# Batch 7's way through memory, in pieces between the layers of the token network, in an attention and mixture-of-depths kernel

## The chip, the cores and the metric

The kernel runs on one core of one Trainium2 chip, in float32. The metric is device time in microseconds (us), from launch to end; lower is better.

A core has five engines, each with its own queue of instructions in a fixed order: PE (matrix products), DVE (vector work, and transposes of 32 x 32 blocks), ACT (activation functions and copies), POOL (vector work, and the DMAs whose rows are picked by an index), SP (all other DMAs here). They wait for each other through semaphores. SBUF is the memory on the core, PSUM the memory that PE writes its products to, DRAM the large one.

## The reference

Attention over 8 batches of 8 heads with queries averaged in pairs, and behind it a mixture of depths: of a batch's 576 rows the 128 with the highest scores go through a two-layer network.

```python
q_pool = q.reshape(B, H, S // 2, 2, D).mean(axis=3)          # B 8, H 8, S 1152, D 64
attn = softmax(q_pool @ k^T / sqrt(D))
x = (attn @ v).transpose(0, 2, 1, 3).reshape(8, 576, 512)
scores = np.einsum('bsd,d->bs', x, w_gate)
out = x.copy()
for b in range(8):
    top_idx = np.argpartition(-scores[b], 128)[:128]
    xe = x[b, top_idx]
    ye = np.maximum(xe @ w1, 0.0) @ w2                        # 512 -> 1024 -> 512
    g = 1.0 / (1.0 + np.exp(-scores[b, top_idx]))
    out[b, top_idx] = x[b, top_idx] + g[:, None] * ye
```

## The kernel before

The order of work on every engine is the order in which the program issues it: the whole of `run` is under a manual schedule, with no planner behind it.

**Attention.** `run` (L1634) goes over 32 pairs of heads, each in two halves of 288 queries. In a half PE makes the scores (L886) and the weighted values of the half before (L904), ACT takes exponents (L893), POOL and DVE the sums. The output rows `x` are stored to `out` in DRAM by SP (L1040).

**Routing.** When a batch's last pair has its scores, a generator `routed(b, part)` (L1074) starts. It issues a few instructions, yields, and is taken up again at set places, so that its pieces stand between other work. Its stages:

- the scores are added up (`line` L1084, `groups` on ACT L955, `total` L961), written to DRAM (L1098) and read back as a line on every partition (L1101);
- ranking: for each of 5 tiles of rows, two DVE passes over the line count how many scores are larger (L1129); POOL and ACT form the gate (L1112, L1142 or L1121, L1145);
- search: which row has rank r. Batches 0 to 6 write rank and gate to DRAM (`row_rank`, L1160), read all of it back to every partition (`lines`, L1164), and let DVE compare (`search`, L1203). Batch 7 instead makes five comparisons (L1173), multiplies them with a table of rows and gates on PE (L1184), turns the result with one more matmul (L1195), and copies index and gate out on ACT (L1196, L1197);
- fetch: POOL gathers the 128 chosen rows from `out` by index (L1230) to `xe`;
- turn: the network needs the rows with features on partitions (`xeT`). Batches 0 to 6 write `xe` to DRAM in an order of its own (L1244), read it back (L1261), and DVE transposes blocks (L1269). Batch 7 is transposed by PE (L1279) and copied by ACT (L1280).

Batches 0 to 5 do all this during the attention, batch 6 mostly; its last pieces and all of batch 7's come in `ending`.

**The network.** The 8 batches are taken in four pairs: (0,1), (2,3), (4,5), (6,7). Each layer of a pair is made as a 2 x 2 product of blocks with seven products instead of eight. The first layer (`first_layer`, L1354) issues seven products of 16 matmuls (L1333), the second (`second_of`, L1426) seven of 8 (L1343). Sums around the products: of the inputs on POOL (`input_sums`, L1319), of the hidden values on DVE (`four_sums`, L1424), and of products on DVE (L1352), with ReLU on ACT (L1368) and copies on ACT (L1370, L1376, L1435, L1437). Every product goes to one of four PSUM tiles, taken in turn (`banks`, L1071); a fifth waits until the first is emptied. At a pair's end DVE scales and adds the result to `xe` (L1347) and POOL scatters it to `out` (`written`, L1302). The hidden quarter c12 is the second operand that the second layer reads, c11 the first.

**The ending.** `ending` (L1456) writes the order out by hand with `pieces(unit, n)`, which takes the next n pieces of a generator: `old` is batch 6's routing, `new` batch 7's, `layer` and `second` pair 0's layers, `third` the next pair's first layer. Pair 0's first layer keeps one product back (`kept`), so that its order is different from the other pairs', and pair 1's first products stand between pair 0's second ones, to fill PE while batch 7 is ranked, searched and turned. Batch 7's routing is done before pair 1 proper begins. In the fourth pair, DVE also checks that all sums of exponents lie in bounds (`counted`, L1592), a small matmul adds the counts (`outside`, L1607), and each engine loads the result (`count_i`, L1560) ahead of the last layer, to branch to a general version if one is out of bounds.

Of the kernel before, what the change touches and what calls it, by code (L numbers as in the profile page):

```python
# [539 lines left out]
class _Plain:  # L540
# [85 lines left out]
    def constants(self):  # L626
# [27 lines left out]
        self.meta = self.const.tile([P, self.NT], F32, name="meta")  # L654
        nc.gpsimd.tensor_scalar(
            out=self.meta[:, :],
            in0=self.token[:, :],
            scalar1=float((self.B - 1) * self.Sp),
            scalar2=None,
            op0=ALU.add,  # L660
        )

# [407 lines left out]

    def banks(self):  # L1071
        return self.psum.tile([P, 2, 512], F32, name="ps")

    def routed(self, b, part):  # L1074
# [33 lines left out]
        if b < self.B - 2:  # L1108
            yield True
        gate = ffn.tile([P, NT], F32, name="gate")  # L1110
# [9 lines left out]
        if b == self.B - 1:  # L1120
            nc.scalar.activation(gate[:, :], gate[:, :], AF.Exp, scale=-1.0)  # L1121
            yield True
        rank = ffn.tile([P, NT], F32, name="rank")
        cuts = {self.B - 2: (1,), self.B - 1: (NT,)}.get(b, (1, 3))
        for t, rows in tiles:
# [12 lines left out]
            if t == cuts[0] < cuts[-1]:  # L1138
                yield True
# [8 lines left out]
        if b == self.B - 1:  # L1148
            meta = self.late[:, self.Dm : self.Dm + NT * BLK].rearrange("p (t n) -> p t n", n=BLK)
            nc.gpsimd.memset(meta, 0.0)  # L1150
            nc.gpsimd.tensor_copy(meta[:, :, 0], self.meta[:, :])
            nc.vector.reciprocal(meta[:, :, 1], gate[:, :])
            nc.vector.tensor_reduce(rank[:, :], parts[:, :, :], AX.X, ALU.add)
        else:

            both = ffn.tile([P, 2, NT], F32, name="both")
            nc.vector.reciprocal(both[:, 1, :], gate[:, :])
            nc.vector.tensor_reduce(both[:, 0, :], parts[:, :, :], AX.X, ALU.add)
            row = self.dram.tile([P * 2 * NT], F32, name="row_rank")
            nc.sync.dma_start(  # L1160
                row.rearrange("(p x) -> p x", p=P), both.rearrange("p a t -> p (a t)")
            )
            lines = ffn.tile([P, P, 2, NT], F32, name="lines", bufs=1)
            nc.sync.dma_start(lines.rearrange("p i a t -> p (i a t)"), _rows_of(row[:], P))  # L1164

        for s0, w in self.slots:
            index = ffn.tile([P, 1], I32, name="index", bufs=self.B)
            own_gate = ffn.tile([P, 1], F32, name="own_gate", bufs=self.B)
            if b == self.B - 1:

                pick = ffn.tile([P, NT, P], F32, name="pick", bufs=1)
                for t, rows in tiles:
                    nc.vector.tensor_scalar(  # L1173
                        out=pick[0:rows, t, 0:w],
                        in0=self.token_line[0:rows, 0, s0 : s0 + w],
                        scalar1=rank[0:rows, t : t + 1],
                        scalar2=None,
                        op0=ALU.is_equal,
                    )
                yield True  # L1180
                ps = self.banks()[:, 0, :]
                n = P // BLK
                for t, rows in tiles:
                    nc.tensor.matmul(  # L1184
                        ps[t % n * BLK : (t % n + 1) * BLK, 0:w],
                        lhsT=meta[0:rows, t, :],
                        rhs=pick[0:rows, t, 0:w],
                        start=(t < n),
                        stop=(t >= NT - n),
                    )  # L1190
                found = ffn.tile([P, NT, P], F32, name="pick", bufs=1)[:, 0, 0:w]
                nc.scalar.copy(found, ps[:, 0:w])
                yield True
                ps = self.banks()[:, 0, 0:2]
                nc.tensor.matmul(ps[0:w, :], lhsT=found, rhs=self.same[:, 0:2], start=True, stop=True)  # L1195
                nc.scalar.copy(index[0:w, :], ps[0:w, 0:1])  # L1196
                nc.scalar.copy(own_gate[0:w, :], ps[0:w, 1:2])  # L1197
            else:
                yield True

                def search(of, to):
                    at = ffn.tile([P, NT, P], F32, name="pick", bufs=1)
                    nc.vector.scalar_tensor_tensor(  # L1203
                        out=at.rearrange("p t i -> p (t i)").rearrange("p (i t) -> p i t", t=NT)[0:w],
                        in0=lines[0:w, :, 0, :],
                        scalar=self.token[0:w, s0 // P : s0 // P + 1],
                        in1=of[0:w, :, :],
                        op0=ALU.is_equal,
                        op1=ALU.mult,
                        accum_out=to[0:w, :],  # L1210
                    )

                found = self.small.tile([P, 1], F32, name="found_token")
                search(self.token_line.rearrange("p t i -> p i t"), found)
                nc.vector.tensor_scalar(
                    out=index[0:w, :],
                    in0=found[0:w, :],
                    scalar1=float(b * Sp),
                    scalar2=None,
                    op0=ALU.add,  # L1220
                )
                if b == self.B - 2:
                    search(lines[:, :, 1, :], own_gate)

                yield True
            if b == self.B - 1:
                xe = ffn.tile([P, self.Dm], F32, name="lines", bufs=1)
            else:
                xe = ffn.tile([P, self.Dm], F32, name="xe", bufs=self.paired + 1)
# [10 lines left out]
            if b != self.B - 1:  # L1240

                n = P // BLK
                copy = self.dram.tile([n, P, P], F32, name="copy")
                nc.sync.dma_start(  # L1244
                    copy[:, 0:w, :].rearrange("a s m -> s a m"), xe[0:w, :].rearrange("s (a m) -> s a m", a=n)
                )
            if b < self.B - 2:
                search(lines[:, :, 1, :], own_gate)
            if b < self.paired:
                xeT = ffn.tile([P, self.ND, P], F32, name="xeT", bufs=self.paired)  # L1250
            if b != self.B - 1:
                yield True
                moved = []

                def read():
                    if b == self.B - 2:
                        moved.append(self.early[:, self.Dm : 2 * self.Dm])
                    else:
                        room = ffn.tile([P, NT, P], F32, name="pick", bufs=1)
                        moved.append(room.rearrange("p t n -> p (t n)")[:, 0 : self.Dm])  # L1260
                    nc.sync.dma_start(moved[0], copy.rearrange("a (j b) m -> (a j) (b m)", b=n))  # L1261

                if b < self.B - 2:
                    self.behind_keys.append(read)
                else:
                    xeT = self.lines_of(self.early[:, 0 : self.Dm])
                    read()
                yield "sums" if b < self.B - 2 else True
                nc.vector.transpose(  # L1269
                    xeT.rearrange("p c (j b) -> p c b j", b=n),  # L1270
                    moved[0].rearrange("p (b i c) -> p c b i", b=n, c=self.ND),
                )
            else:
                yield mid
                xeT = self.lines_of(self.late[:, 0 : self.Dm])
                pv = self.banks()[:, 0, :].rearrange("p (c n) -> p c n", n=P)
                of = xe.rearrange("p (n c) -> p c n", c=self.ND)
                for c in range(self.ND):
                    nc.tensor.transpose(pv[:, c, 0:w], of[0:w, c], self.ident[0:w, 0:w])  # L1279
                nc.scalar.copy(xeT[:, :, 0:w], pv[:, 0 : self.ND, 0:w])  # L1280
# [30 lines left out]
    def input_sums(self, a, s):  # L1311

        a11, a12, a21, a22 = a
        s1, s2, s3, s4 = s
        add, subtract = ALU.add, ALU.subtract
        for i, (to, x, y, op) in enumerate(
            ((s1, a21, a22, add), (s2, s1, a11, subtract), (s3, a11, a21, subtract), (s4, a12, s2, subtract))
        ):
            self.nc.gpsimd.tensor_tensor(out=to, in0=x, in1=y, op=op)  # L1319
            if i % 2:  # L1320
                yield
# [32 lines left out]
    def first_layer(self, a, s, c, m, kept=None):  # L1354


# [15 lines left out]
        ps = product(a12, b21)  # L1372
        yield
        hidden(c11, u, ps)
# [10 lines left out]
        if kept is None:  # L1385
            hidden(c21, u, product(a22, t4))
            yield
# [68 lines left out]
    def ending(self, halves, old):  # L1456
# [6 lines left out]
        def pieces(unit, n=None):  # L1463
            for i, _ in enumerate(unit):
                if i + 1 == n:
                    break
# [308 lines left out]
```

## Time and profile before

| | |
|---|---|
| device time, three runs | 678.05, 680.55, 680.17 us, median 680.17 |
| the profiled execution's own time | 678.44 us |
| its span (first to last instruction) | 676.6 us |
| granted PE clock | 0.998 of full |
| attention's last product on PE begins | 559.66 us (140 matmuls shown from there) |
| pair 0's first product | 568.26 us |
| batch 7: `line` on DVE, gather on POOL, transposes on PE | 575.07, 593.48, 598.13 us |
| last product on PE | 667.39 us, 16 matmuls in 3.62 us |

The span counts from the first instruction of the program; the device time has a little more around it (678.44 against 676.6). "PE" rows are matmuls, "x16" means sixteen of them in the row's time; a bracket at a row's end is the idle time before it and what ended it. "SPq" and "POOLq" are the sequencers of SP and POOL, which issue DMAs.

### The profile page before, as it was taken

Reading aid. Unit: us, or ns where it says so; the run is one execution under the profiler, and the core shown is the slowest. Engines: PE = TensorE matmul, PEld = TensorE weight load, DVE = VectorE, ACT = ScalarE, POOL = GpSimd, SP = SyncE. Lnnn points to the kernel's source line nnn. Section 1 sums busy time; section 2 is a strip of 40 time slices with the busy share of each in tenths; the row PEclk is TensorE's granted clock in tenths of the full one; section 3 lists DMA queues with packets and bytes.
Section 4 is the critical chain, followed back from the end, with each engine's and each line's share of the span. In section 5 each row is a group of like instructions: output and inputs, shape, how many; then the busy total and the mean of one; then the engine's idle time right before and its main releaser. Section 6 shows DMA issues by size and latency. Waiting matters only on the chain.

```text
span 676.6 us, 23416 instructions
## 1 busy us (share of the span) xinstructions
PE 668.3 (99%) x9951; PEld 445.9 (66%) x9951; DVE 564.1 (83%) x824; ACT 448.2 (66%) x978; POOL 502.7 (74%) x476
## 2 busy tenths in 40 slices
PE   9999999999999999999999999999999999999996
PEld 5656666666666666666666666656666667899995
DVE  4878898998999888998799889988998897865464
ACT  6677777777877777777777777777777773321210
POOL 5888888889888978898889988898889878230211
PEclk9999999999999999999999999999999999999999
DMA  8799999858885788768885788678958744310000
GB/s 162 145 199 184 203 183 192 159 106 186 159 161 100 138 166 164 136 116 163 153 166 110 157 153 154 127 148 157 153 127 151 156 132 133 61 48 16 17 32 35
DMA packets 390089, 91.51 MB, mean 135 GB/s; under 512 B 371416, under 2 KB 375384, under 8 KB 389976
## 3 DMA queue, kind: packets, MB, share of 16 engines
q1 hardware_dynamic: 388536, 85.54, 65.8%
q0 software_dynamic: 1280, 4.20, 1.7%
q8 instruction: 79, 1.29, 0.9%
q14 instruction: 34, 0.28, 0.2%
q10 hardware_dynamic: 160, 0.20, 0.1%
HBM read 74.38 MB, written 15.52 MB: 133 GB/s over the span
## 4 chain that ended last, share of the span: by engine, by line
PE 94%; issue 2%; DVE 1%; DMA 1%; POOL 1%; ACT 0%; POOLq 0%; ACTq 0%; DVEq 0%
PE ps L886 42%; PE ps L904 41%; PE ps L1343 5%; PE ps L1333 5%; DMA p<-in_q_dram 0%; POOL p L1319 0%; DMA out_dram<-lines,index 0%; DVE p L1352 0%; POOL prod L993 0%; DVE acc L1352 0%; PE ps L1184 0%; POOL out_dram L1302 0%; PE ps L852 0%; DVE x L1029 0%; ACT groups L955 0%
## 5 line engine op out<-in xcount | busy, mean ns | idle before, releaser
L893 ACT ACTIVATE p<-ps 128x576 f32<-128x576 f32 x576 | 320.8, 694 | 2.7 <-PE ps L886 2.6
L925 POOL TENSOR_TENSOR acc<-p 128x576 f32<-128x576 f32 x192 | 283.1, 1503 | 37.8 <-ACT p L893 37.1
L886 PE MATMUL ps<-qT,kT 64*64 64x288 f32 x4608 | 292.5, 403 | 0.2
L904 PE MATMUL ps<-p,v_sb 64*64 64x288 f32 x4608 | 291.0, 403 | 0.0
L886 PEld LDWEIGHTS ps<-qT,kT 64*64 64x64 f32 x4608 | 174.0, 133 | 106.1 <-ACT p L893 14.6
L904 PEld LDWEIGHTS ps<-p,v_sb 64*64 64x64 f32 x4608 | 172.9, 133 | 106.8 <-ACT p L893 14.9
L930 DVE TRANSPOSE_TENSOR_REDUCE fold<-p 128x54 f32<-128x1728 f32 x64 | 126.2, 1972 | 45.7 <-ACT p L893 45.6
L912 ACT COPY two<-ps 128x576 f32<-128x576 f32 x64 | 41.0, 640 | 132.0 <-PE ps L904 129.5
L930 DVE TRANSPOSE_TENSOR_REDUCE fold<-acc 128x54 f32<-128x1728 f32 x64 | 124.4, 1943 | 4.4 <-POOL acc L925 4.4
L914 POOL TENSOR_TENSOR av<-two 128x288 f32<-128x288 f32 x64 | 51.4, 803 | 39.4 <-ACT two L912 38.7
L774 DVE STREAM_TRANSPOSE kT<-kb 128x1152 f32<-128x1152 f32 x31 | 73.5, 2372 | 0.0
L993 POOL TENSOR_TENSOR prod<-avb,w_gate 128x288 f32<-128x288 f32 x64 | 51.8, 809 | 0.0
L771 POOL TENSOR_TENSOR qp<-qb 128x576 f32<-128x576 f32 (+1 forms) x32 | 43.9, 1374 | 5.7 <-DMA qb<-in_q_dram 5.7
L1129 DVE TENSOR_SCALAR_CACHE_REDUCE pick<-line 128x127 f32<-128x127 f32 (+4 forms) x80 | 45.2, 565 | 2.3
L1302 POOL DMA_INDIRECT out_dram<-xe,index x7 | 7.0, 994 | 47.4 <-DVE xe L1347 38.5
L970 ACT ACTIVATE sums<-total,tiny 32x18 f32<-32x18 f32 x124 | 38.3, 309 | 1.9
L1029 POOL TENSOR_TENSOR x<-avb,rec 128x576 f32<-128x576 f32 x30 | 34.8, 1160 | 0.0
L983 DVE STREAM_TRANSPOSE avb<-av 128x288 f32<-128x288 f32 x64 | 28.4, 444 | 3.2 <-POOL av L914 3.2
L1368 ACT ACTIVATE p<-p 128x512 f32<-128x512 f32 x16 | 10.1, 632 | 31.6 <-DVE p L1352 31.6
L1051 DVE TENSOR_REDUCE red<-prod 128x9 f32<-128x288 f32 x64 | 27.8, 435 | 2.7 <-POOL prod L993 2.7
L955 ACT COPY groups<-sum 32x36 f32<-32x36 f32 x124 | 27.3, 220 | 2.2 <-DVE sum L940 0.7
L779 DVE STREAM_TRANSPOSE qT<-qp 128x576 f32<-128x576 f32 (+1 forms) x32 | 23.4, 732 | 0.7 <-POOL qp L771 0.7
(131 smaller groups left out, 434.7 us busy)
## 6 DMA issues: line engine op xcount, KB each, us to landing
kb<-in_k_dram SPq DMA_DIRECT2D x124, 144.0 KB, 4.8
qb<-in_q_dram SPq DMA_DIRECT2D x124, 144.0 KB, 4.7
v_sb<-in_v_dram SPq DMA_DIRECT2D x31, 576.0 KB, 5.8
out_dram<-x SPq DMA_DIRECT2D x128, 72.0 KB, 5.0
lines<-row_rank SPq DMA_DIRECT2D x7, 640.0 KB
w<-in_moe_w_dram SPq DMA_DIRECT2D x8, 512.0 KB
line<-gate_lines SPq DMA_DIRECT2D x8, 351.5 KB
tw<-tw SPq DMA_DIRECT2D x4, 512.0 KB
```

The lines of the kernel that those rows point to most:

```text
L771: nc.gpsimd.tensor_tensor(out=qp[:, of, :], in0=pair["q"][:, of, 0, :], in1=pair["q"][:, of, 1, :], op=ALU.add)
L774: nc.vector.transpose(kT.rearrange("p (c i g) -> p c g i", c=self.NC, i=BLK), pair["k"].rearrange("p (g c) d -> p c g d", c=self.NC),)
L886: nc.tensor.matmul(sc[keys, j, 0:n], lhsT=pair["kT"][rows, c * P + keys.start : c * P + keys.stop], rhs=pair["qT"][rows, qs], start=True, ...
L893: nc.scalar.activation(p[:, c // G, c % G, :, :], sc[:, :, 0:n], AF.Exp, scale=self.scale)
L904: nc.tensor.matmul(av[j * self.D : (j + 1) * self.D, e, 0:n], lhsT=half["pair"]["v"][keys, j, c, :], rhs=half["p"][keys, c // G, c % G, j, :],
L912: nc.scalar.copy(two[:, :, :], av[:, :, 0:n])
L914: nc.gpsimd.tensor_tensor(out=half["av"][:, :], in0=two[:, 0, :], in1=two[:, 1, :], op=ALU.add)
L925: nc.gpsimd.tensor_tensor(out=acc[:, u, :], in0=units[:, 0, u, :], in1=units[:, 1, u, :], op=ALU.add)
L930: nc.vector.tensor_reduce(fold[:, a, :], of.rearrange("p u (m d) -> p (u m) d", d=BLK), AX.X, ALU.add, apply_transpose=True,)
L970: self.nc.scalar.activation(tot[rows, :], pair["total"][:, j * self.QB : (j + 1) * self.QB], AF.Identity, bias=self.tiny[0:BLK, 0:1],)
L993: self.nc.gpsimd.tensor_tensor(out=pair["prod"][:, ns, :], in0=pair["avb"][:, ns, :], in1=self.w_gate[:, hp : hp + 1, :].broadcast_to([P, ...
L1129: nc.vector.tensor_scalar(out=cmp[0:rows, 0 : part.stop - part.start], in0=near[0:rows, part], scalar1=sc[0:rows, t : t + 1], scalar2=None ...
```

## The change

Batch 7 takes the same way as the other batches: rank and gate to DRAM, lines back, DVE search, gather, copy to DRAM, read back, DVE transpose. The matmuls, the table `meta` and the ACT copies of the other way go. `ending` no longer writes out the order: the routing generators stand in a list `waiting`, and after every piece of a layer `pieces` takes one piece of the first of them. `pause(n)` in `routed` makes batch 7 let n such turns pass. Pair 0 is treated like pairs 1 and 2, in one loop: first layer, one piece of the second, `four_sums`, next pair's `input_sums`, the other pieces. `first_layer` has no `kept` product any more, and seven pieces instead of eight. Before the third pair's last pieces, whatever is left of the routing is issued at once.

```diff
+    def pause(self, n):
+        for _ in range(n):
+            yield True
...
         yield True
         if b < self.B - 2:
             yield True
+        if b == self.B - 1:
+            yield from self.pause(3)
         gate = ffn.tile([P, NT], F32, name="gate")
...
-        if b == self.B - 1:
-            nc.scalar.activation(gate[:, :], gate[:, :], AF.Exp, scale=-1.0)
-            yield True
         rank = ffn.tile([P, NT], F32, name="rank")
-        cuts = {self.B - 2: (1,), self.B - 1: (NT,)}.get(b, (1, 3))
+        cuts = {self.B - 2: (1,), self.B - 1: (0, 1, 2, 3)}.get(b, (1, 3))
...
-            if t == cuts[0] < cuts[-1]:
+            if t in cuts[:-1]:
                 yield True
...
         for s0, w in self.slots:
...
-                for t, rows in tiles:
-                    nc.tensor.matmul(
-                        ps[t % n * BLK : (t % n + 1) * BLK, 0:w],
-                        lhsT=meta[0:rows, t, :],
-                        rhs=pick[0:rows, t, 0:w],
...
+            yield True
             if b == self.B - 1:
+                yield from self.pause(4)
...
             if b == self.B - 1:
-                xe = ffn.tile([P, self.Dm], F32, name="lines", bufs=1)
+                xe = self.late[:, self.Dm : 2 * self.Dm]
...
+            if b < self.B - 2:
+                self.behind_keys.append(read)
             else:
-                yield mid
-                xeT = self.lines_of(self.late[:, 0 : self.Dm])
-                pv = self.banks()[:, 0, :].rearrange("p (c n) -> p c n", n=P)
-                of = xe.rearrange("p (n c) -> p c n", c=self.ND)
-                for c in range(self.ND):
-                    nc.tensor.transpose(pv[:, c, 0:w], of[0:w, c], self.ident[0:w, 0:w])
-                nc.scalar.copy(xeT[:, :, 0:w], pv[:, 0 : self.ND, 0:w])
+                read()
+            yield "sums" if b < self.B - 2 else True
+            if b == self.B - 1:
+                yield from self.pause(3)
+            nc.vector.transpose(
+                xeT.rearrange("p c (j b) -> p c b j", b=n),
+                moved[0].rearrange("p (b i c) -> p c b i", b=n, c=self.ND),
+            )
...
-    def first_layer(self, a, s, c, m, kept=None):
+    def first_layer(self, a, s, c, m):
...
-        ps = product(a12, b21)
-        yield
-        hidden(c11, u, ps)
+        hidden(c11, u, product(a12, b21))
...
-        if kept is None:
-            hidden(c21, u, product(a22, t4))
-            yield
+        hidden(c21, u, product(a22, t4))
+        yield
         hidden(c12, w, product(s4, b22))
         yield
-        if kept is not None:
-            copy(kept, product(a22, t4))
-            yield
-            hidden(c21, u, kept)
-            yield
...
+        waiting = [old]
 
         def pieces(unit, n=None):
             for i, _ in enumerate(unit):
+                while waiting and next(waiting[0], None) is None:
+                    waiting.pop(0)
                 if i + 1 == n:
                     break
...
         self.gated(halves[-3])
-        pieces(old, 1)
+        next(old)
...
-        pieces(layer, 1)
+        pieces(following[4], 1)
         self.normalized(last)
         self.gated(halves[-1])
         self.scored(halves[-1])
         _, new, _ = self.routing.pop()
-        pieces(old, 1)
-        pieces(new, 1)
-        pieces(layer, 3)
+        waiting.append(new)
+        pieces(following[4], 1)
         for of in (halves[-3]["pair"], last):
             self.divided(of)
             self.stored(of)
-        pieces(layer, 1)
-        pieces(old)
-        pieces(layer, 1)
-        pieces(new, 1)
-        pieces(layer, 2)
...
-        for i in range(1, self.B // 2 - 1):
+
+        for i in range(1, self.B // 2):
             tokens, c, s, _, layer = following
             pieces(layer)
-            following = layers(i + 1, rooms[(i + 1) % 2], m[(i + 1) % 2])
-            pieces(self.input_sums(*following[3]))
             second = self.second_of(tokens, c, s, acc[1])
-            pieces(second, 3)
+            pieces(second, 1)
             self.four_sums(c, s)
+            if i == self.B // 2 - 1:
+                while waiting:
+                    for _ in waiting.pop(0):
+                        pass
+            following = layers(i, rooms[i % 2], m[i % 2])
+            self.input_sums(*following[3])
             pieces(second)
 
         (six, seven), c, s, _, third = following
         pieces(third, 4)
         low = self.counted()
         pieces(third, 2)
         count = self.outside(low)
-        pieces(third, 1)
         self.four_sums(c, s, slice(0, 3))
         pieces(third)
         self.four_sums(c, s, slice(3, 4))
```

## The prediction

> **What bounds the kernel now.** First the page's busy shares and the chain that ended last, then each engine's timeline from 568 us on. The order of instructions, which lists for both kernels what stands on each engine and which semaphores it waits for, shows that up to there nothing moves except one small POOL instruction (`meta`) that goes.
>
> ```profile
> PE 668.3 (99%) x9951; PEld 445.9 (66%) x9951; DVE 564.1 (83%) x824; ACT 448.2 (66%) x978; POOL 502.7 (74%) x476
> PE 94%; issue 2%; DVE 1%; DMA 1%; POOL 1%; ACT 0%; POOLq 0%; ACTq 0%; DVEq 0%
> ```
>
> PE works 99% of the span, so only what PE executes, or waits for, sets the time. I number a pair's products F1 to F7 (first layer) and S1 to S7 (second layer) in PE's order; the layers multiply pair 0 from 568.26. PE's timeline:
>
> ```profile
> 568.26 2.05 PE L1333 MATMUL ps<-xeT,w 128*128 128x128 f32 x16
> ...
> 581.09 1.89 PE L1343 MATMUL ps<-w,p 128*128 128x256 f32 x8
> 583.63 1.99 PE L1343 MATMUL ps<-w,p 128*128 128x256 f32 x8 [0.64 <-ACT p L1368]
> ...
> 589.67 1.23 PE L1184 MATMUL ps<-pick,v_sb 128*32 128x128 f32 x10 [0.54 <-ACT acc L1435]
> 590.83 2.05 PE L1333 MATMUL ps<-xeT,w 128*128 128x128 f32 x16
> 592.72 0.28 PE L1195 MATMUL ps<-same,pick 128*128 128x2 f32 x2
> ...
> 598.13 0.63 PE L1279 MATMUL ps<-ident,lines 128*128 128x128 f32 x4
> ...
> 621.34 3.73 PE L1333 MATMUL ps<-xeT,w 128*128 128x128 f32 x32
> ...
> 645.94 3.73 PE L1333 MATMUL ps<-v_sb,w 128*128 128x128 f32 x32
> ```
>
> Pair 2 runs from 621.34 to 645.94 without a gap: 24.60 us for 14 products, an F step being 1.79 and an S step 1.725. Pairs 0 and 1 take 53.08 (568.26 to 621.34); two clean pairs and one small matmul (0.14) would take 49.34. The surplus of 3.74 is batch 7's own matmuls (start to next start 1.16 + 0.14 + 0.47 = 1.77), two waits (0.64 + 0.54), and 0.79 of switching. So 3.74 us is the most that the change can win.
>
> [...] a scatter is confirmed 2.7 us after issue, and the next one on POOL starts 3.5 to 4.7 us after it. [...] PE here has no idle above 0.64[...].
>
> **What goes and is hidden.** Batch 7's ten matmul calls leave PE, four copies leave ACT, five `is_equal` (1.06 in all) leave DVE. Two searches come (1.32 and 0.78 at the median, 2.13 and 1.85 at worst) in pair 1's first layer, where DVE waited 1.8 us for PE at a time. Four DMA issues come on SP, which had nothing after the stores. POOL's input sums for pair 2 stand behind the gather, needed some 20 us later. All at nothing.
>
> **Wait A: pair 0's second product.** Pair 0's first layer is no longer interleaved, and on DVE batch 6's transpose, batch 7's scores, two divisions and the first ranking tile now stand ahead of the last sum (c12) that S2 reads. DVE and SP before:
>
> ```profile
> 576.27 0.26 DVE L961 TENSOR_REDUCE total<-groups 32x18 f32<-32x72 f32 x1 [0.92 <-ACT groups L955]
> 579.78 1.14 DVE L1269 STREAM_TRANSPOSE v_sb<-v_sb 128x512 f32<-128x512 f32 x1
> 582.22 0.69 DVE L1352 TENSOR_TENSOR p<-acc,ps 128x512 f32<-128x512 f32 x1
> ```
>
> ```profile
> 569.22 0.38 SPq L1244 DMA_DIRECT2D copy<-xe  x1
> 573.10 0.33 SPq L1261 DMA_DIRECT2D v_sb<-copy  x1
> ```
>
> The new order on DVE, with start-to-start steps of before: the first sum at 575.07; batch 6's transpose at 575.9 (its read, issued 573.10, moves bytes until 575.5 in half-microsecond windows[...]); `line` +1.03 = 576.93; `total` +1.20 (by way of ACT) = 578.13; two divisions from +0.20 = 578.33 to 579.67; u 579.67, w +0.77, c22 +0.77, u +0.60, c21 +0.77 = 582.58; memsets to 583.44. The ranking's line lands at total + 0.29 + 1.34 + 3.38 = 583.14, no wait. One tile of ranking 1.24: c12 at 584.68. From c12's sum to S2 is 1.41 (582.22 to 583.63): S2 at 586.09 instead of 581.09 + 1.73 = 582.82. A = 3.27, bounds 2.9 and 3.8 by the landings. The ranking tiles after it (2 x 1.25) end before S4 needs its sums.
>
> **Wait B: batch 7's turn.** In the new order batch 7's gather waits for both scatters of pair 0 (before, it ran ahead of them), and batch 7's transpose stands on DVE just ahead of the four sums of pair 1, so PE's S4 waits for it. The POOL rows that price it:
>
> ```profile
> 593.48 1.11 POOL L1230 DMA_INDIRECT lines<-out_dram,index  x1 [8.35 <-ACT own_gate L1197]
> 601.75 1.04 POOL L1302 DMA_INDIRECT out_dram<-xe,index  x1 [7.16 <-DVE xe L1347]
> 605.45 1.00 POOL L1302 DMA_INDIRECT out_dram<-xe,index  x1 [2.66 <-DVE kT L1352]
> 622.76 0.99 POOL L1302 DMA_INDIRECT out_dram<-xe,index  x1 [13.36 <-DVE xe L1347]
> 627.49 0.98 POOL L1302 DMA_INDIRECT out_dram<-xe,index  x1 [3.74 <-PE ps L1333]
> ```
>
> With A, pair 1's F1 starts at 586.09 + 6 x 1.725 = 596.44. A pair's first scatter starts 1.42 after the next F1 (621.34 to 622.76): 597.86. From scatter to scatter it is 3.70, 4.73 and 3.49, mean 3.97; I use it twice: scatter 601.83, gather 605.80. Gather to copy is 3.47 (565.75 on POOL to 569.22), copy to read 3.88, read to landing 2.8: 615.95. Transpose 1.03, first sum 0.67, handover 0.05: S4 at 617.70. Without waiting it would be 596.44 + 7 x 1.79 + 3 x 1.725 = 614.15. B = 3.55; 2.3 with the shorter gap and quicker landing, 5.5 with two gaps near 4.7. The ranking's way to the search (row out about 593.1, lines back about 598.4, as before 4.7 us at most) is not the later one: index by 601.
>
> Pair 2 then starts at 617.70 + 4 x 1.725 = 624.60 against 621.34: +3.26.
>
> **Wait C: the count.** The scans of `sums` (2 x 0.79) now follow the fourth product's sums instead of filling an idle gap, and `found` stands behind c21. In before's clock: w 654.07, scans 654.68, c22 656.26, u 656.86, c21 657.63, `found` 658.23, `count_i` done 658.72. PE loads it ahead of S1:
>
> ```profile
> L1560 PEldq TENSOR_LOAD <-count_i x1: 489/489/489, 656.8 to 656.8; - x1
> ```
>
> Load 0.49 and 0.2 to issue: S1 at 659.4 instead of 658.76. C = 0.65, bounds 0.3 and 1.0. The tail after PE stays.
>
> **Sum.** 3.26 + 0.65 = +3.9. The profiled execution took 678.44 (span 676.6), so 682.3 there; the median shown is 680.17, so 684.1.
>
> **Rivals.**
> - Batch 7 hides (B is nothing). Not slower by what can be measured: if the gather starts on its index (601 or earlier) its turn is over near 612, before 614. Then -0.3 + 0.65, about 680.5. Against: the gather's semaphores include the second scatter's queue. It decides from gather at 602.2 or earlier.
> - Both A and B vanish, if DVE's steps pack closer than before's: -3.7 + 0.65, 677.1. For: the 3.74 of surplus is real. Against: A is DVE work in order, with hardly any idle in it.
> - Slow transfers: the gather takes 6.1 to landing (its median in the whole trace), the read 5.8 (same), so +5.6: 689.7. For: those are the medians. Against: they were beside loads, and the queues are empty here.[...]
> - The change not doing what it says: the drain before the third pair finds nothing left, since batch 7's turn stands in the second pair; no time in that.
>
> **How the numbers follow.** A measurement of this kernel tells about 0.5% (3.4 us) from no change. Forecast 0.72 (its own range 682.4 to 686.6; five sixths of it past 683.6, as what I left out, clock and landings, adds rather than takes), slow transfers 0.10, hidden 0.14, both vanish 0.04. Slower 0.60 + 0.10 = 0.70; same 0.12 + 0.14 = 0.26; faster 0.04. For 8 in 10 the range reaches from the hidden case, about 680.5, to part of the slow one, 688.2.
>
> **What would show it.** Right: PE idle about 3.3 before S2 of pair 0, waiting for ACT `p`, and about 3.5 before S4 of pair 1, with DVE waiting for the DMA of `pick` there; two scatters ahead of the gather on POOL; PE idle half a microsecond before pair 3's S1; no waits in pair 2. Wrong: a gather right after the index, or DVE with idle inside A.

## The result, and the profile after

The changed kernel takes 682.76 us (median of 21 runs, 680.0 to 685.53) against 679.22 for the kernel before in the same rounds (21 runs, 677.7 to 681.09). The ratio is 1.0052, with a 95% interval of 1.004 to 1.0065: about half a per cent slower, +3.5 us, where +3.9 was forecast. The profiled execution took 683.74 with a span of 681.9 (before 678.44 and 676.6). That is 1.0 above the mean of its 21 runs, while the profiled execution of before was 0.8 under the mean of its own, so the two traces differ by 5.3 and the runs by 3.5. Why is part of what follows.

The page of the kernel after: PE's busy share, the row of its granted clock, and the shares of the chain that ended last.

```profile
PE 669.4 (98%) x9935; PEld 447.0 (66%) x9935; DVE 566.8 (83%) x825; ACT 446.7 (66%) x973; POOL 501.9 (74%) x473
PEclk9999999999999999999999999999999999799999
PE 87%; issue 4%; DMA 4%; POOL 1%; DVE 1%; SPq 1%; ACT 0%; POOLq 0%; DVEq 0%; ACTq 0%
```

The page counts 16 PE instructions fewer, and PE is busy 1.1 us longer. DMA has gone from 1% to 4% of the chain. The clock row, all 9 before, has one slice of 17 us at 7 instead of 9. PE's timeline of the kernel after (start, busy time, operation, and in brackets the idle time before it; L1281 is the first layer, L1291 the second, L1525 the small matmul of the count):

```profile
568.59 2.05 PE L1281 MATMUL ps<-xeT,w 128*128 128x128 f32 x16
...
581.42 1.89 PE L1291 MATMUL ps<-w,p 128*128 128x256 f32 x8
585.96 3.78 PE L1291 MATMUL ps<-w,p 128*128 128x256 f32 x8 [2.65 <-ACT p L1314]
589.54 3.20 PE L1291 MATMUL ps<-kT,p 128*128 128x256 f32 x8
...
599.48 3.73 PE L1281 MATMUL ps<-xeT,w 128*128 128x128 f32 x32
...
615.44 1.89 PE L1291 MATMUL ps<-kT,p 128*128 128x256 f32 x8
618.62 1.96 PE L1291 MATMUL ps<-kb,p 128*128 128x256 f32 x8 [1.29 <-DVE p L1362]
...
625.61 2.62 PE L1281 MATMUL ps<-xeT,w 128*128 128x128 f32 x22
...
650.20 2.06 PE L1281 MATMUL ps<-v_sb,w 128*128 128x128 f32 x17
...
661.13 2.05 PE L1281 MATMUL ps<-p,w 128*128 128x128 f32 x16
663.75 1.96 PE L1291 MATMUL ps<-w,p 128*128 128x256 f32 x8 [0.57 <-PE ps L1281]
```

The three waits stand where they were forecast:

- A: S2 of pair 0 could begin at 583.15 (581.42 + 1.73) and begins at 585.96, so 2.81.
- B: S4 of pair 1 could begin at 617.19 (615.44, when S3 begins, + 1.73, with rounding) and begins at 618.62, so 1.43.
- C: S1 of pair 3 could begin at 662.92 (661.13 + 1.79) and begins at 663.75, so 0.83.

Pair 2 has none: 625.61 to 650.20 is 24.59, as before.

A fourth loss is not idle time. S2 of pair 0 takes 3.58 to the next product's start and S3 3.03, instead of 1.73 each: 3.15 us while PE counts as busy. The view by windows of the same execution (window, its length, busy time and instructions of five engines, then PE's granted clock, DMA share, GB/s) shows why:

```profile
584.50:585.00 0.50, 0.00 (x0) 0.00 (x0) 0.50 (x3) 0.00 (x0) 0.50 (x1) 1.00 0.63 97
585.00:585.50 0.50, 0.00 (x0) 0.00 (x0) 0.50 (x2) 0.22 (x1) 0.50 (x2) 0.84 0.68 104
585.50:586.00 0.50, 0.04 (x1) 0.04 (x1) 0.46 (x3) 0.50 (x2) 0.50 (x2) 0.50 0.86 135
586.00:590.00 4.00, 4.00 (x10) 3.19 (x11) 3.89 (x10) 0.39 (x2) 0.43 (x1) 0.50 0.15 26
592.00:592.50 0.50, 0.50 (x3) 0.39 (x3) 0.46 (x4) 0.00 (x0) 0.00 (x0) 0.83 0.00 0
592.50:593.00 0.50, 0.50 (x4) 0.43 (x3) 0.00 (x0) 0.23 (x1) 0.00 (x0) 1.00 0.00 0
```

PE's clock falls to half while it idles in A, about 2 us after its last work, and comes back near 592.2: some 6.8 us at half speed, of which PE works 6.2 (585.96 to 592.2) and so loses half of that. From here on this is called a closing of the clock; the expectations below also speak of the gate that closes.

With the starts these sum as follows. The first product begins 0.33 later than before. Pairs 0 and 1 take 57.02 (568.59 to 625.61) instead of 53.08: the clean 49.34, A 2.81, the clock 3.15, B 1.43, and 0.29 that is left over. C adds 0.83. Together 0.33 + 3.94 + 0.83 = 5.1; the last product on PE begins 5.07 later (672.46 instead of 667.39).

### The profile page after: what moved, and what is told of

The parts are those of the page before. It is cut to its first block, busy times and chain, and to the rows that moved or that the text cites. A ratio compares the mean times of both kernels' runs of the same rounds, so it can differ in the third digit from the quotient of the medians.

```text
span 681.9 us, 23388 instructions
## 1 busy us (share of the span) xinstructions
PE 669.4 (98%) x9935; PEld 447.0 (66%) x9935; DVE 566.8 (83%) x825; ACT 446.7 (66%) x973; POOL 501.9 (74%) x473
## 4 chain that ended last, share of the span: by engine, by line
PE 87%; issue 4%; DMA 4%; POOL 1%; DVE 1%; SPq 1%; ACT 0%; POOLq 0%; DVEq 0%; ACTq 0%
PE ps L895 41%; PE ps L877 41%; PE ps L1281 3%; PE ps L1291 3%; DMA out_dram<-xe,index 1%; POOL p L1269 1%; DMA p<-in_q_dram 1%; DMA v_sb<-out_dram,index 1%; DMA line<-gate_lines 1%; SPq L801 0%; DMA out_dram<-v_sb,index 0%; DMA pick<-copy 0%; DMA copy<-v_sb 0%; DVE v_sb L1227 0%; DVE kT L1300 0%
## 5 line engine op out<-in xcount | busy, mean ns | idle before, releaser
L1123 DVE TENSOR_SCALAR_CACHE_REDUCE pick<-line 128x127 f32<-128x127 f32 (+4 forms) x80 | 45.2, 564 | 2.3
L1291 PE MATMUL ps<-w,p 128*128 128x256 f32 x96 | 24.2, 403 | 3.2 <-ACT p L1314 2.7
```

The source lines that it names most:

```text
L1123: nc.vector.tensor_scalar(out=cmp[0:rows, 0 : part.stop - part.start], in0=near[0:rows, part], scalar1=sc[0:rows, t : t + 1], scalar2=None ...
L1291: self.nc.tensor.matmul(to, lhsT=of[:, k, :], rhs=by[:, k, :], start=k == 0, stop=k == n - 1)
```

## The experiments

All are edits of the changed kernel. Theory T1 is the reading above: A's idle, B near 1.4, C near 0.8, and the closed clock on top. T2 is the forecast's own pricing: no cost from the clock, and B near 3.5. Where a T3 is named, it puts the loss outside these places, so that moving the pieces brings little back. The table gives medians, the ratio to the kernel before in the same rounds with its 95% interval, and the difference of the means from that kernel, with a 95% interval too. The means are there because the runs of both kernels fall in two clumps (last section), so that a median can jump between them.

| kernel | runs | median us | ratio | mean minus mean of before, us |
|---|---|---|---|---|
| the change | 21 | 682.76 | 1.0052 (1.004 to 1.0065) | +3.56 ± 0.8 |
| the change again, later | 10 | 681.66 | 1.0037 (1.0023 to 1.0052) | +2.80 ± 0.9 |
| e1 ranking one piece later | 22 | 680.57 | 1.0011 (1.0003 to 1.002) | +0.89 ± 0.5 |
| e2 turn three pieces later | 22 | 680.59 | 1.0016 (1.0005 to 1.0027) | +1.23 ± 0.6 |
| e3 count one piece earlier | 8 | 681.77 | 1.0038 (1.0021 to 1.0056) | +2.20 ± 1.2 |
| e6 A's idle filled, five matmul calls | 22 | 681.63 | 1.0027 (1.0018 to 1.0036) | +1.84 ± 0.4 |
| e10 A's idle filled, two calls | 22 | 681.35 | 1.0027 (1.0017 to 1.0037) | +1.77 ± 0.6 |
| e7 e6 and e2 together | 13 | 680.04 | 1.0004 (0.9993 to 1.0015) | +0.28 ± 0.7 |
| e4 e1, e2 and e3 together | 9 | 677.71 | 0.9968 (0.9954 to 0.9982) | -1.89 ± 0.7 |
| e5 e4, and divisions later | 6 | 676.6 | 0.9952 (0.9936 to 0.9969) | -2.62 ± 1.1 |
| e9 e5, and search two pieces later | 6 | 675.92 | 0.995 (0.9932 to 0.9968) | -3.31 ± 1.2 |

The change itself stands at +3.3 ± 0.6 over its 31 runs ((21 x 3.56 + 10 x 2.80) / 31), and single edits are read against that. The intervals of the gains below hold the noise of both sides.

**e1: A, by its last cause.** The whole ranking moves behind c12's sum, and the search stays in its place.

```diff
         if b == self.B - 1:
-            yield from self.pause(3)
+            yield from self.pause(4)
...
             if b == self.B - 1:
-                yield from self.pause(4)
+                yield from self.pause(3)
```

> The changed kernel with batch 7's ranking taken up one piece later, so that its first tile (memsets and tile: 583.21 to 584.56 on DVE, 1.35 us) stands behind the sum c12 instead of ahead of it. Theory 1 (wait A of 2.8 us is mostly DVE order, and its idle closes PE's clock gate for 6.8 us in most runs, which costs another 3.2): A falls to about 1.4, the gate stays open, mean clock 0.998 or more in every run; 682.8 - 1.4 - 2.3 (3.2 in some 7 of 10 runs) = about 679. Theory 2 (waits alone, as forecast, A 3.3, B 3.55): only 1.4 is won, 681.4.

It came out between the two, 2.4 ± 0.8 under the change (3.3 - 0.9). PE's timeline of e1:

```profile
582.81 1.89 PE L1291 MATMUL ps<-w,p 128*128 128x256 f32 x8
585.96 1.99 PE L1291 MATMUL ps<-w,p 128*128 128x256 f32 x8 [1.26 <-ACT p L1314]
...
616.12 1.97 PE L1291 MATMUL ps<-kb,p 128*128 128x256 f32 x8 [1.84 <-DVE p L1362]
```

A is halved: 1.42 from 584.54 to 585.96. S2 runs at its full pace again. B has grown to 2.0, which is what T1 left out: DVE's ranking now ends at 594.8, ahead of the last sums of pair 0, and so the first scatter on POOL starts 2.06 after pair 1's first product (598.48 against 596.42), not 1.42. The gather behind it is later by as much. The sum agrees: 1.4 of idle and some 1.5 of clock won (e6 and e10 below), 0.6 of B lost.

One expectation failed. Six of the 22 runs have a mean clock of 0.997 or less, where 0.998 or more was expected in all. Five have 0.997, which stands in 8 of 115 runs of the kernel before too; the sixth has 0.996, which none of those has. So the clock may still close now and then in e1, in A's 1.26 us of idle or in B's 1.84. The trace of e1 shows no closing, so which of the two it would be stays open.

**e2: B, by its place.** The transpose of batch 7 is issued three pieces later.

```diff
             if b == self.B - 1:
-                yield from self.pause(3)
+                yield from self.pause(6)
             nc.vector.transpose(
```

> The changed kernel with batch 7's transpose taken up three pieces later, behind pair 1's four sums. Wait B (S4 of pair 1) should go: in the trace it is 1.4 us. Theory 1: 1.4 won, 681.3, clock still about 0.994 to 0.996 in most runs. Theory 2 (B worth 3.55, as forecast): 679.2.

The gain was 2.1 ± 0.9 (3.3 - 1.2), again between; T1's 1.4 lies in the interval, T2's 3.6 does not. B is gone from the trace: the only idle before the third pair is A's 2.64. How much of the 2.1 is B is not clear from this run alone, since the clock still closes in it, for a shorter time in most runs (mean clock 0.997 in 16 of 22, where 0.994 to 0.996 was expected); e7 separates the two.

**e3: C, by its place.**

```diff
-        pieces(third, 4)
+        pieces(third, 3)
         low = self.counted()
         pieces(third, 2)
         count = self.outside(low)
+        pieces(third, 1)
```

> The changed kernel with the scans of the sums and the count put back to where they stood before among pair 3's pieces. Wait C should go: both theories 0.6 to 0.8 won, about 682.0, the idle of 0.57 ahead of pair 3's S1 gone, waits A and B as they were.

The wait is gone as expected: no idle is left in the fourth pair. The gain in the mean is 1.1 ± 1.3 from eight runs, so the time alone does not show it. Its profiled execution shows something else: an idle in A as long as in the change, with the clock still open. PE's timeline of e3:

```profile
580.84 1.89 PE L1291 MATMUL ps<-w,p 128*128 128x256 f32 x8
585.38 1.99 PE L1291 MATMUL ps<-w,p 128*128 128x256 f32 x8 [2.65 <-ACT p L1314]
587.21 1.89 PE L1291 MATMUL ps<-kT,p 128*128 128x256 f32 x8
```

So the closing is not certain at 2.65 us. The runs of the change say the same: six of the 21 have a mean clock of 0.999 (mean time 681.29), six 0.996 (682.54), six 0.994 (684.25), and three other values. A half clock for 6.8 us of 682 takes 0.005 off the mean clock, one for half as long 0.0025. The clock also falls to half behind PE's last product: at 673.97 in the trace of before, 2.6 us ahead of the span's end, and at 680.92 in that of the change, 1.0 ahead, which takes 0.0019 and 0.0007 off by itself. The 115 runs of the kernel before, whose trace has no other closing, have mean clocks of 0.997 to 1. So 0.998 to 1 goes with no closing in A, 0.995 to 0.997 with a short one and 0.994 with a long one (0.995 could be either of the two, 0.997 could be none), and the times of the three groups differ by 1.25 and 2.96.

**e6 and e10: the clock without the wait.** Matmuls are added just ahead of S2 of pair 0, into the PSUM tile that S2 then overwrites: five calls, ten instructions, in e6, and two calls, four instructions, in e10. They are no part of the computation. They leave the wait as it is and take only PE's idleness away.

```diff
-    def second_layer(self, a, s, order):
+    def second_layer(self, a, s, order, fill=0):
...
+        for n, i in enumerate(order):
+            ps = self.banks()[:, 0, :]
+            if fill and n == 1:
+                of, by = a11, b11
+                for k in range(fill):
+                    self.nc.tensor.matmul(
+                        ps[0 : of.shape[2], 0 : by.shape[2]],
+                        lhsT=of[:, k % 4, :],
+                        rhs=by[:, k % 4, :],
+                        start=True,
+                        stop=True,
+                    )
...
-            second = self.second_of(tokens, c, s, acc[1])
+            second = self.second_of(tokens, c, s, acc[1], 5 if i == 1 else 0)
```

> The changed kernel with five more matmuls on PE ahead of pair 0's S2, into the same PSUM tile, which S2 then overwrites (2.16 us at 0.43 each): they are not part of the computation and fill most of the idle time of wait A, S2 still starts at the same moment. Theory 1: the gate stays open (clock 0.998 or more in every run), and though PE does more, the median falls by about 2.3 (3.2 in some 7 of 10 runs) to 680.5, and S2 and the next product take 1.73 each instead of 3.58 and 3.03. Theory 2 (no gate, waits alone): no change, 682.8.

> The changed kernel with two added matmuls (not part of the computation) ahead of pair 0's S2 instead of five: 0.9 us of work, so that an idle of about 1.8 is left of the 2.65. It asks how much idle closes the gate. If 1.8 is too short to: clock 0.998 or more in every run and a mean of 681.3, as with five. If it still closes: clocks of 0.997 and less in a good part of the runs and a mean nearer 682.5.

PE's timeline of e6:

```profile
584.66 2.32 PE L1345 MATMUL ps<-w,p 128*128 128x256 f32 x10
587.48 1.99 PE L1291 MATMUL ps<-w,p 128*128 128x256 f32 x8 [0.49 <-ACT p L1314]
589.31 1.89 PE L1291 MATMUL ps<-kT,p 128*128 128x256 f32 x8
```

and of e10:

```profile
583.08 1.03 PE L1345 MATMUL ps<-w,p 128*128 128x256 f32 x4
585.90 1.99 PE L1291 MATMUL ps<-w,p 128*128 128x256 f32 x8 [1.79 <-ACT p L1314]
587.73 1.89 PE L1291 MATMUL ps<-kT,p 128*128 128x256 f32 x8
```

In both S2 still waits 2.82 from the end of S1 (584.66 to 587.48, 583.08 to 585.90). With 2.16 us more work for PE (1.73 for eight instructions, so 2.16 for ten) e6 is 1.5 ± 0.7 faster than the change, and e10 as much (± 0.9). T2, in which the clock costs nothing, had no gain for e6. That gain is the clock's price, but for some 0.3: B is 1.15 and 1.27 in these two traces instead of 1.43, as the gather landed sooner. An estimate from the clocks agrees: of the change's 31 runs six have a long closing (0.994, at 3.15) and 16 a short one (0.995 to 0.997, at the 1.7 that the next trace shows), which is 46 us, or 1.5 a run. T1 had put it higher (2.3), as it reckoned with a long closing in 7 of 10 runs. All 22 runs of each have a mean clock of 0.998 or more. So an idle of 1.8 us did not close the clock once in 22 runs, while 2.65 did in at least 13 of 21 runs of the change (those with a mean clock of 0.996 or less), and in 8 of 10 when it was run again.

**The change again.** The changed kernel ran ten more times, later.

> The changed kernel itself, on the same chip as these runs: 682.8 in the mean, and its runs spread over the mean clocks 0.994 to 0.999, the higher clock with the shorter time. Theory 2 (no gate): no relation of clock and time.

Its mean is 682.15, and time goes with clock: eight runs at 0.995 or 0.996 have a mean of 682.5, two at 0.998 or more one of 680.75. T2 had no such relation. The windows of its profiled execution, columns as above:

```profile
586.00:587.00 1.00, 0.00 (x0) 0.00 (x0) 0.96 (x4) 0.61 (x2) 1.00 (x3) 0.94 0.77 120
587.00:588.00 1.00, 0.93 (x2) 0.83 (x3) 0.96 (x3) 0.28 (x2) 0.47 (x1) 0.50 0.60 95
590.00:590.50 0.50, 0.50 (x3) 0.39 (x3) 0.50 (x2) 0.00 (x0) 0.00 (x0) 0.70 0.00 0
590.50:591.00 0.50, 0.50 (x4) 0.45 (x3) 0.50 (x2) 0.33 (x1) 0.00 (x0) 1.00 0.00 0
```

Here the clock is at half from about 586.9 to 590.3, 3.4 us, half as long as in the first trace. S2 takes 3.41 (587.07 to 590.48), and S3 its 1.72: 1.7 lost rather than 3.15. The same idle (2.64) closes the clock for a short or a long time, or not at all.

**e7: B without the clock.** e6's matmuls and e2's later transpose.

> The changed kernel with the five added matmuls (not part of the computation) that hold PE busy in wait A, and the transpose three pieces later. The gate is open with and without the late transpose, so the difference to the run with the added matmuls alone (681.3 in the mean) is wait B alone. Theory 1 (B 1.0 to 1.4, as the traces show): 680.1. Theory 2 (B 3.55, as forecast): 677.8.

The mean is 1.56 ± 0.8 under e6's (1.84 - 0.28), with a mean clock of 0.998 or more in all of e6's runs and in 12 of these 13. That is B, and it agrees with the 1.43 of the change's trace and the 1.15 of e6's, not with the forecast's 3.55.

**e4: all three places.** The diffs of e1, e2 and e3 together.

> The changed kernel with three edits at once: ranking one piece later, transpose three pieces later, count put back. Theory 1 (waits A 2.8, B 1.4, C 0.8 and the clock gate, which A's idle closes): of A 1.4 is left, B and C are gone, the gate stays open: the clean order's gain of 3.7 less 1.4 = 2.3 faster than before, 677.2. Theory 2 (the single edits' gains in the mean, 2.4 + 2.1 + 1.1 against the changed kernel's 682.8, add up): the same 677.2, so this run tells whether they do. Theory 3 (what the single edits won was largely one and the same thing, the gate): not below 679.

It fell where T1 and T2 have it in common, and against T3: 5.2 ± 0.9 us come back in the mean (3.3 + 1.9), near the sum of the single edits (2.4 + 2.1 + 1.1 = 5.6). Only A's other half is left in PE's timeline of e4:

```profile
582.15 1.89 PE L1291 MATMUL ps<-w,p 128*128 128x256 f32 x8
585.28 1.99 PE L1291 MATMUL ps<-w,p 128*128 128x256 f32 x8 [1.24 <-ACT p L1314]
```

**e5: A's first half.** The two divisions on DVE (1.35 in all) and the stores behind them move from ahead of pair 0's sums to behind its four sums.

```diff
-        for of in (halves[-3]["pair"], last):
-            self.divided(of)
-            self.stored(of)
-
...
             self.four_sums(c, s)
+            if i == 1:
+                for of in (halves[-3]["pair"], last):
+                    self.divided(of)
+                    self.stored(of)
```

> As the run with three edits, and the two divisions with their stores moved behind pair 0's four sums, so that DVE reaches c12 about 1.3 us earlier. Theory 1: wait A falls to about 0.1, all of the 3.7 us of the clean order is won: 675.9 against before's 679.5, PE without any idle over 0.3 from pair 0's first product on. Theory 3: still not below 679. A cost of the way through memory itself, if there is one that no wait shows, would keep it above 677.

No idle is left before S2 of pair 0, and yet the median is 0.7 above the expected time. The stores now stand on SP ahead of the write of the ranks, which goes out at 596.58 instead of 593.87 in the change. DVE's timeline of e5 has the consequence:

```profile
602.43 1.35 DVE L1161 SCALAR_TENSOR_TENSOR pick<-lines,token,token_line 128x640 f32<-128x640 f32 x1 [2.62 <-DMA lines<-row_rank]
```

The search waits 2.62 for its lines, and DVE's sums behind it are late: PE idles 0.38 in pair 1's first layer (at 604.64).

**e9: the search later.** e5, and the search two pieces later, behind more sums.

```diff
             if b == self.B - 1:
-                yield from self.pause(3)
+                yield from self.pause(5)
```

> As the run with four edits, and batch 7's search two pieces later. In that run the stores, moved back, stood ahead of the ranks on SP (row out 596.58, lines at 602.4), DVE waited 2.6 us for the lines at the search, and PE lost about 0.9 around pair 1's F6 and S1. Theory 1 (nothing but such waits separates the kernel from the clean order): 675.9 in the mean, no idle of PE over 0.3 from pair 0's first product to the last. Theory 3 (a cost of the way through memory that no wait shows): no better than the 676.7 of the run with four edits.

The time is as expected. PE's timeline of e9 has S1 and S2 of pair 0 in one row, and one wait of 0.60 where none over 0.3 was expected:

```profile
582.45 3.80 PE L1291 MATMUL ps<-w,p 128*128 128x256 f32 x16
...
609.72 1.99 PE L1291 MATMUL ps<-w,p 128*128 128x256 f32 x8 [0.60 <-ACT p L1314]
```

On DVE the second search (0.88) now stands just ahead of the last sums that this product reads. The median is the lowest of all: 0.5% under the kernel before (0.995, interval 0.9932 to 0.9968), 6.6 ± 1.3 under the change in the mean (3.3 + 3.3). That e9 beats e5 is not shown, with six runs of each (0.7 ± 1.5).

## Why the prediction was right, and what in it was not

The total was right, +3.9 against +3.5, and so were the direction and the places of all waits. Part of this is luck, two errors that cancel: B too large by 2.1, and a price of nothing for the clock, which is 1.5 in the mean. A and B both lie under the forecast's own bounds (2.9 to 3.8, 2.3 to 5.5). The absolute figure, 684.1, stood on a median of three runs, 680.17, where 21 give 679.22.

**The clean order.** The forecast let the removed matmuls and switches win at most 3.74. e9, which keeps the way through memory and has 0.60 of waiting left, wins 3.3. So that term holds, and the way through memory itself costs nothing that shows beside the ± 1.2 of that mean: the loss was in the places of its pieces on DVE and in the clock.

**A, forecast 3.27, found 2.81.** The mechanism is the forecast one. DVE's timeline of the kernel after has the first ranking tile (L1123) directly ahead of c12's sum:

```profile
583.43 0.34 DVE L1123 TENSOR_SCALAR_CACHE_REDUCE pick<-line 128x127 f32<-128x127 f32 x1
...
583.82 0.81 DVE L1123 TENSOR_SCALAR_CACHE_REDUCE pick<-line 128x576 f32<-128x576 f32 x1
...
584.56 0.68 DVE L1300 TENSOR_TENSOR p<-acc,ps 128x512 f32<-128x512 f32 x1
```

c12 begins at 584.56, forecast 584.68. Most of the difference in A is that PE's own products began 0.33 later, which the wait absorbs. e1 and e5 split A as the forecast built it: the ranking tile (2.81 - 1.42 = 1.4), and the divisions (1.40, from 583.88 to 585.28, the wait that e4 still has and e5 has not). The first trace of after also shows no wait for the ranking's line, as forecast. The 0.4 that the forecast has from the last bytes of batch 6's read (575.5) to its transpose (575.9) was an estimate; here the transpose begins at 575.88, directly behind the first sum. Batch 7's transpose, which does wait for its read, begins 0.3 behind the half-microsecond window that holds the last bytes (616.5, 616.82).

**The clock: the term that failed.** "At nothing" was right for the moved steps, but A's idle of 2.8 has a consequence on the resource that bounds the kernel, and the sum had no term for it. In the first trace of the change the clock is at half (0.50) for 6.8 us, in the second for 3.4, and 2.65 us of PE idleness was enough for it in most runs (a mean clock of 0.996 or less in 13 of 21).

"PE here has no idle above 0.64" holds between the products and leaves out what comes behind them. The trace of before has the closing at its end, where PE's last product is over at 671.01. Its windows (columns as above):

```profile
673.00:674.00 1.00, 0.00 (x0) 0.00 (x0) 0.00 (x0) 0.00 (x0) 0.00 (x0) 0.98 0.67 258
674.00:675.00 1.00, 0.00 (x0) 0.00 (x0) 0.00 (x0) 0.00 (x0) 0.00 (x0) 0.50 0.05 12
```

It begins shortly before 674, 3.0 us after PE's last work, so that 3.0 us without work can halve the clock was there to be seen before the forecast was made. The price in the mean is what e6 and e10 win back, 1.5 us (1.0 to 1.8, as the change is taken from its second or its first group of runs); 1.7 and 3.15 in these two executions of the change, which were traced with the clock closed. What makes the difference between 2.65 us with a closing and without one (e3) is not shown.

**B, forecast 3.55, found 1.43 in the trace and 1.56 by e7.** The mechanism is right: gather behind both scatters, transpose ahead of the four sums. The chain of waits of the kernel after (start, length, what), cut to its steps:

```profile
600.90 2.84 DMA out_dram<-xe,index
...
604.53 2.88 DMA out_dram<-xe,index
...
608.21 3.67 DMA v_sb<-out_dram,index
611.90 2.29 DMA copy<-v_sb
...
614.24 2.56 DMA pick<-copy
...
616.82 1.11 DVE v_sb L1227
617.93 0.56 DVE p L1362
...
618.62 5.42 PE ps L1291 x24
```

The first scatter starts 1.42 after pair 1's first product (600.90 against 599.48), as forecast. The wrong term is copy to read, 3.88 in the sum and 2.34 here (611.90 to 614.24): 1.54 of the 2.1. It came from batch 6's copy in the trace of before; in the trace after, the same copy takes 3.37 (issued at 569.71 and 573.08). The other six copies of before, beside loads, took 3.88 to 4.46 to their reads, so no row there was nearer to 2.34. The forecast had written that the queues would be empty here, and priced the step all the same by a copy that was not alone. These are the DMA queues while batch 6's copy of before is under way (569.22 to 573.10; packets, MB, share of the 16 DMA engines):

```profile
q1 hardware_dynamic: 528, 0.26, 24.2%
q8 instruction: 1, 0.02, 1.5%
```

and while batch 7's copy is (611.90 to 614.24, the kernel after):

```profile
q1 hardware_dynamic: 528, 0.26, 35.3%
```

Beside batch 6's copy one packet of instructions (16 KB) is moved. The copy ends in 16 completions of 4 bytes: 15 are there 1.94 us after its issue, as with batch 7's copy, where all 16 are, and the last one only 3.41 after it. In the trace of the change it is the same: the packet and one late completion (2.89 after the issue) with batch 6's copy, and neither with batch 7's. That the packet is what holds up that last part is argued from this, not shown. The two gaps after the scatters are 3.63 and 3.68 rather than 3.97 each (0.63 together), the mean of three that included one that had waited for something else (4.73). Gather to copy, 3.69 for 3.47, goes the other way. Read to landing, 2.8 in the sum, is 2.56.

**C, forecast 0.65, found 0.83**, inside its bounds; e3 shows that it is the place of the count. DVE has `count_i` done at 662.89 in the kernel after, PE's sequencer loads it then, and S1 begins some 0.35 after the load (663.75), where the forecast had 0.2 (the trace of before has 0.20 behind the same load on POOL's sequencer, 657.31 to 657.51):

```profile
L1478 PEldq TENSOR_LOAD <-count_i x1: 491/491/491, 662.9 to 662.9; - x1
```

The edits costed at nothing held: the search did not wait, and pair 2 has no wait.

**The rivals.** The gather did wait for the second scatter (2.54 idle on POOL before it), so B did not hide, but at 1.43 it came nearer to that than its price of 3.55 says. The slow transfers did not come; the closing of the clock came without them.

Not tried: the old way of batch 7 (its matmuls on PE) in the new order of layers, and a gather ahead of the scatters.

## What to carry to other kernels

An idle gap of PE, where PE bounds the kernel, costs more than its length if the clock closes in it: here 1.8 us was free of that in all 22 runs of e10 and 2.65 mostly was not, so a sum of waits needs a term for it, and a gap that long is the first to shorten. Wherever a trace has the clock at half, the end of the program included, it shows an idle time that was enough there (2.0 us in the first trace of the change, 3.0 at the end of before). When small work is spread between the steps of a pipeline, look at what stands directly ahead of the one instruction for which the bounding engine waits: here one ranking tile, two divisions, a search, a transpose and a count, moved by some pieces, turned +0.5% into -0.5% with the same work. A DMA step has to be priced from a case with the same traffic beside it: a pair of issues with one packet of instructions beside them was off by two thirds for a pair without (3.88 for 2.34).

## What the runs showed of the hardware

- The closing of the clock varies with the same idle: for 6.8 us in one trace (the change), 3.4 us in two (the change again and e2), not at all in a fourth (e3), with 2.64 to 2.65 us of PE idle in each. It begins 2.0, 2.5 and 2.9 us after PE's last work ahead of the wait. The third of these, in e2, is 0.26 us after PE had begun again (587.30 against 587.04), so the idle can be over when the clock falls.
- At the end of the program, where nothing follows, the clock falls to half 3.0 us after PE's last product in the trace of before (671.01, 673.97) and 4.85 in that of the change (676.07, 680.92).
- The runs of both kernels fall in two clumps, some 2 us apart (the kernel before near 678.3 and 680.1, the change at a mean clock of 0.994 near 683.7 and 685.3). At least part of it is older than all the change touches: the first sixteen score matmuls take 1.20 us in some executions and 2.20 in others, and all behind them is shifted. PE's timeline of the change when it was run again:

```profile
6.75 2.20 PE L877 MATMUL ps<-qT,kT 64*64 64x288 f32 x16
```

and of its first execution:

```profile
6.15 1.20 PE L877 MATMUL ps<-qT,kT 64*64 64x288 f32 x16
```

  The granted clock reads 1.00 in the windows from 6 to 9 us of both, so the record of the clock doesn't show it. What decides between the two is open.
- On quiet queues the DMA steps repeat closely: batch 7's copy takes 2.34 us from its issue to the read behind it in the traces of the change, e1, e2, e5 and e9, and in the same traces it is 3.5 to 3.7 from a scatter to the next indexed DMA on POOL where that waits for nothing else (4.5 and 5.7 in e5 and e9, where the second scatter stands behind a late search).
